# A cyclic order for five engines, rebuilt: attention pairs, routing steps and both remainder copies in an attention + mixture-of-experts kernel

## The chip, the cores and the metric

The kernel runs on one core of a Trainium2 chip. The metric is the device time of one execution, in microseconds (us). Names of engines: PE is TensorE (matrix products and transposes), DVE is VectorE, ACT is ScalarE, POOL is GpSimd, SP is SyncE, which here issues nearly all transfers.

## The reference

Attention with rotary positions over 8 batches, 8 heads, 576 tokens and 64 dimensions a head, then a layer in which each of the 4608 tokens goes through one of 8 experts.

```python
q_rot, k_rot = rotate(q), rotate(k)
scores = q_rot @ k_rot.T / sqrt(64)
scores = scores - scores.max(-1)
attn = exp(scores) / (sum(exp(scores)) + 1e-9)
x = (attn @ v) laid out as 4608 tokens x 512
logits = x @ w_gate                       # 8 experts
e = argmax(logits); g = softmax(logits)[e]
out = g * (relu(x @ w1[e]) @ w2[e])       # everything in float32
```

## The kernel before

Two heads make a **pair**; there are 32 pairs (`npair`), four to a batch. The attention part runs as a software pipeline. `PLAN` (line 26) is a list of steps `(token, offset)`; `window(w)` (line 769) walks it once and performs every token for pair `w - offset`. So one window holds one pair's worth of work, taken from up to seven neighbouring pairs. The last letter of a token is its engine (p PE, v DVE, a ACT, g POOL, d a transfer issued by SP). `chained_emit` (line 727) ties the instructions of each engine together in the order of the list, so that `PLAN`, read engine by engine, is the order in which each engine works. Every engine and SP's queue work strictly in order.

The tokens, in the order in which one pair goes through them:
- `FQd`, `FKd` fetch the pair's q and k (`fetch`, line 376). `paced` (line 368) makes such a load wait for the ACT instruction that stood last in the order.
- `RQg`, `RKg` rotate q and k on POOL (line 395, then the sum on line 396).
- `HQa`, `HKa` round q and k on ACT, `LQg`, `LKg` form the rests on POOL; `DHd`, `DLd` copy the halves of q across partitions.
- `cR` copies the last 64 columns of the rotated q into `zq` (line 409 is the helper's line of every copy), `DRd` swaps them across partitions.
- `S0p` to `S8p` are the nine score blocks on PE (six products each, line 459; S4, the remainder rows, line 454). They go into the PSUM tile `sp`, of which there are two.
- `M0v` to `M8v` on DVE copy a block out of PSUM, negated, and take its row maximum (line 471); `E0a` to `E8a` on ACT are the exponentials with their row sums (line 478).
- `TA0p`, `TA1p`, `TB0p`, `TB1p` transpose the exponentials on PE (line 496), `TRp` those of the remainder (lines 503, 507). Each fills one PSUM tile `tp`; there are two of these, handed out in turn to TR, the four T, the output block O and the products V.
- `cA0a` to `cB1a` copy the four T blocks to `PT` on ACT. TR is copied in two parts: `c1v` on DVE takes its first 256 columns to `PT`, `c2` the other 256 to `PR` (512 elements a partition each). `c3v` copies two small blocks out of O. c1 and c2, with c3, are the remainder copies.
- `V0p` to `V8p` multiply by v (lines 540, 542), `Uv` copies the result, `Op` (line 568) brings it to token rows and multiplies by the gate's weights, `X0v`, `X1v` (line 592) scale it into the batch's tile `xt`.
- `ZDd` moves a pair's remainder row sums across partitions (line 485); `RZv` on DVE sums and inverts the row sums (lines 145, 554) and so waits for `ZDd`.

Once a batch has its four pairs, **gating** (`gate`, line 620) routes its tokens: `gL` logits, `gM` maximum, `gD` difference (POOL, line 651), `gE` exponential (ACT, line 654), `gG`, `gW` weight, `gQ`, `gB`, `gO` one-hot, `gP` counts on PE inside O, `gR` ranks, `gU` (POOL, line 701), `gY` list positions. Then come five stores of the batch's rows (`gS0d` to `gS4d`, SP, line 671) and five scatters of the token lists (`gI0g` to `gI4g`, POOL, line 709). `GATE`, `STORES` and `LISTS` say after which token of which later window each of these goes.

From pair 28 on, `route_first` spreads the first steps of the expert schedule over the windows, `first_slots` loads three index lists through SP, the first expert's weights are loaded (lines 892, 894) and the first tokens gathered (line 322). As the pairs run out, the expert part begins: slots of 256 tokens with one expert each, PE at work all the time (lines 959 and 991). It takes the second half of the time.

Of the kernel before, what the change touches and what calls it, by code (L numbers as in the profile page):

```python
# [35 lines left out]
]  # L36
GATE = [
    ("gLv", 2, "G1"), ("gMv", 2, "G1"), ("gDg", 2, "RQg"), ("gEa", 2, "E6a"), ("gGv", 2, "G2"), ("gWv", 2, "G2"),
    ("gQv", 2, "G3"), ("gBv", 2, "G3"), ("gOv", 3, "G1"), ("gUg", 4, "RQg"), ("gYv", 4, "G2"),
]  # L40
STORES = (
    [
        ("gS0d", 3, "GS"), ("gS1d", 4, "GS"), ("gS2d", 5, "GS"), ("gS4d", 5, "ZDd"), ("gS3d", 6, "GS"),
    ],
    [
        ("gS0d", 3, "FQd"), ("gS1d", 3, "ZDd"), ("gS2d", 3, "FKd"), ("gS3d", 3, "DHd"), ("gS4d", 3, "DLd"),
    ],
)
LISTS = (
    [  # L50
        ("gI0g", 5, "GI"), ("gI1g", 6, "GI"), ("gI2g", 7, "GI"), ("gI3g", 8, "GI"), ("gI4g", 8, "LKg"),
    ],
    [
        ("gI0g", 4, "RKg"), ("gI1g", 5, "LQg"), ("gI2g", 5, "GI"), ("gI3g", 5, "RQg"), ("gI4g", 5, "LKg"),
    ],
)
W0 = -4
WARM = 80
RSTEP = ("M8v", "X0v", "M5v", "M1v", "Uv", "M6v", "M0v")
WSPLIT = (("TB0p", "cA1a"), ("HQa", "HKa"))  # L60
CHUNK = (0, 1, 3, 4, 2)
NR = 2
# [19 lines left out]
def kernel(  # L82
# [11 lines left out]
    B, H, S, D = v.shape  # L94
# [741 lines left out]
    WT = npair + max(off for tok, off in PLAN if tok[0] == "T")  # L836
# [94 lines left out]
    def keep(f, *a):  # L931
        chained_emit(lambda: f(*a), True)
# [103 lines left out]
    def early(i):  # L1036
        return {k: (lambda g=g: split1(g)) for g, k in enumerate(WSPLIT[i], 2 * i)}
# [168 lines left out]
```

## Time and profile before

| | |
|---|---|
| Median of 3 runs | 975.3 us (975.07 to 978.81) |
| The profiled execution | 973.34 us |
| Its span, first to last instruction | 971.2 us |
| PE, weight loads, DVE, ACT, POOL busy | 923.0, 778.2, 666.7, 665.9, 480.0 us |
| Mean granted TensorE clock | 0.971 of full speed |

The profile's summary adds up busy time over the whole span. The questions here are about one pair of some 13 us, so the views to read are those of a stretch: the table of waits, the table of windows, and the order of time on one engine. A row in order of time gives the start, the length, the engine, the line, the result and the operands with their shapes, how many instructions are merged, and in brackets how long the engine was idle before it and what released it. PE's instructions overlap, so the distance from one start to the next, not the length, is what a group costs PE.

### The profile page before, as it was taken

The page shows a single profiled execution, that of the slowest core. Times are in us where ns is not written, and L with a number is a line of the kernel's source. Part 1 is how long each engine was busy: PE and PEld are TensorE (multiplying, and loading weights), DVE is VectorE, ACT ScalarE, POOL GpSimd, SP SyncE. Part 2 cuts the span into 40 slices and gives each one's busy share as a digit, 9 for nine tenths or more (in the row PEclk, how much of TensorE's full clock was granted, in tenths as well). Part 3 has the DMA queues.
Part 4 walks back from the last instruction along what each step waited for, and adds up shares of the span by engine and source line. Part 5 has one row for each costly group of instructions (what it writes and reads, how often), then busy time and mean ns, then how long its engine had stood idle before and what let it go on. Part 6 is the DMA issues. An engine that isn't in the chain of part 4 may idle for free. (4 is left out here: it accounts for less than half of the span.)

```text
span 971.2 us, 25315 instructions
## 1 busy us (share of the span) xinstructions
PE 923.0 (95%) x9656; PEld 778.2 (80%) x9656; DVE 666.7 (69%) x1382; ACT 665.9 (69%) x1185; POOL 480.0 (49%) x335
## 2 busy tenths in 40 slices
PE   5799999999999999998999999999999999999997
PEld 4577777777777777765688999999999999997886
DVE  6557777777777777785478565666666666667987
ACT  2689999899998999887444445455445555456875
POOL 5977879998989889870224122222222111110111
PEclk7679999999999999999799999999999999999999
DMA  6656666676666766655312377414425311155991
GB/s 231 169 152 191 182 189 184 158 198 176 174 178 164 189 175 184 167 132 186 121 24 81 94 238 232 150 62 146 144 68 173 117 48 47 43 184 182 371 336 58
DMA packets 99827, 152.95 MB, mean 157 GB/s; under 512 B 28791, under 2 KB 62263, under 8 KB 99696
## 3 DMA queue, kind: packets, MB, share of 16 engines
q1 hardware_dynamic: 91408, 128.86, 45.6%
q0 software_dynamic: 8000, 21.20, 6.6%
q8 instruction: 79, 1.29, 0.6%
q10 hardware_dynamic: 288, 1.18, 0.3%
q14 instruction: 52, 0.43, 0.2%
HBM read 162.49 MB, written 23.80 MB: 192 GB/s over the span
## 5 line engine op out<-in xcount | busy, mean ns | idle before, releaser
L471 DVE TENSOR_SCALAR_CACHE_REDUCE pn<-sp 128x576 f32<-128x576 f32 x256 | 186.4, 746 | 34.5 <-PE sp L459 29.8
L478 ACT ACTIVATE pn<-pn,negm 128x576 f32<-128x576 f32 x256 | 195.1, 768 | 2.2 <-DVE pn L471 2.2
L459 PE MATMUL sp<-k,q 64*128 64x288 f32 x1536 | 168.0, 331 | 11.0 <-DMA q<-q 8.9
L959 PE MATMUL hp<-xh,w1h 128*128 128x256 f32 x544 | 154.4, 284 | 0.7 <-issue 0.4
L959 PE MATMUL hp<-xl,w1h 128*128 128x256 f32 x544 | 154.2, 283 | 0.0
L959 PE MATMUL hp<-xh,w1l 128*128 128x256 f32 x544 | 153.9, 283 | 0.0
L459 PEld LDWEIGHTS sp<-k,q 64*128 64x128 f32 x1536 | 118.5, 198 | 26.3 <-issue 17.5
L898 DVE TENSOR_TENSOR w2l<-r,w2h 128x1024 fp32r<-128x1024 f32 x92 | 111.7, 1231 | 36.3 <-ACT w2h L897 31.1
L1001 POOL DMA_INDIRECT out_dram<-y,gi x34 | 34.4, 1011 | 204.0 <-DVE y L152 181.2
L542 PE MATMUL tp<-PT,vn 128*64 128x320 f32 (+1 forms) x1024 | 134.5, 414 | 0.0
L409 ACT COPY PT<-tp 128x1024 f32<-128x1024 f32 x128 | 125.0, 1013 | 13.5 <-PE tp L496 12.3
L991 PE MATMUL yp<-w2h,hh 128*128 128x512 f32 x320 | 126.5, 395 | 0.0
L991 PE MATMUL yp<-w2h,hl 128*128 128x512 f32 x320 | 124.9, 390 | 0.0
L991 PE MATMUL yp<-w2l,hh 128*128 128x512 f32 x320 | 124.8, 390 | 0.0
L898 DVE TENSOR_TENSOR w1l<-r,w1h 128x1024 fp32r<-128x1024 f32 x96 | 113.0, 1217 | 4.3 <-ACT w1h L897 3.6
L542 PEld LDWEIGHTS tp<-PT,vn 128*64 128x64 f32 x1024 | 71.8, 139 | 48.8 <-issue 6.8
L959 PEld LDWEIGHTS hp<-xh,w1h 128*128 128x128 f32 x544 | 104.3, 192 | 2.4 <-DVE lpi L145 0.6
L959 PEld LDWEIGHTS hp<-xh,w1l 128*128 128x128 f32 x544 | 104.3, 192 | 0.6
L959 PEld LDWEIGHTS hp<-xl,w1h 128*128 128x128 f32 x544 | 104.3, 192 | 0.6 <-issue 0.5
L395 POOL TENSOR_TENSOR qk<-qk,rotq 128x1152 f32<-128x1152 f32 x31 | 82.1, 2648 | 45.4 <-DMA qk<-in_qk_dram 42.2
L496 PE MATMUL tp<-cst,pn 64*128 64x64 f32 x2048 | 91.2, 231 | 13.7 <-ACT pn L478 8.5
L927 ACT ACTIVATE hh<-hp 128x512 fp32r<-128x512 f32 x68 | 40.6, 598 | 90.0 <-PE hp L959 86.2
(192 smaller groups left out, 1775.6 us busy)
## 6 DMA issues: line engine op xcount, KB each, us to landing
r<-in_moe_w_dram SPq DMA_DIRECT2D x192, 512.0 KB
qk<-in_qk_dram SPq DMA_DIRECT2D x64, 576.0 KB
q<-q SPq DMA_DIRECT2D x128, 128.0 KB
x_dram<-xt SPq DMA_DIRECT2D x32, 288.0 KB
vn<-in_v_dram SPq DMA_DIRECT2D x32, 256.0 KB
xlist<-mark SPq DMA_DIRECT2D x8, 289.0 KB
x_dram<-xt SPq DMA_DIRECT2D x8, 144.0 KB
zq<-zq SPq DMA_DIRECT2D x64, 16.0 KB
```

What stands on the lines that cost most here:

```text
L395: e.tensor_tensor(out=x, in0=x, in1=rot, op=ALU.mult)
L409: (nc.scalar.copy if eng == "a" else nc.vector.tensor_copy)(out=o, in_=i)
L459: nc.tensor.matmul(sp[:, u, 0:HS], lhsT=st["q"][r, int(h != u), qp, i * P:(i + 1) * P], rhs=st["k"][r, kp, h], start=(i_ == 0), stop=(i_ = ...
L471: nc.vector.tensor_scalar(out=scores(st, n, j), in0=st.pop(("S", j))[:, :, 0:HS], scalar1=-1.0, scalar2=None, op0=ALU.mult, op1=ALU.min, a ...
L478: nc.scalar.activation(out=t, in_=t, func=AF.Exp, bias=st["negm"][:, j:j + 1], scale=-1.0, accum_out=zs[n % 4][:, CHUNK[i], h, 0:1])
L496: nc.tensor.transpose(tp[:, b, c:c + 64], pns[n % 2][r, i, k:k + P], ident[r, r])
L542: nc.tensor.matmul(o, lhsT=st["vn"][:, h, s % 4, :], rhs=st["PT"][:, h, s % 4, x:x + w], start=(s % 4 == 0), stop=False)
L898: nc.vector.tensor_tensor(out=lo, in0=src, in1=hi.bitcast(F32), op=ALU.subtract)
L927: nc.scalar.activation(out=hh, in_=hp, func=AF.Relu)
L959: m = nc.tensor.matmul(hp[:, fi], lhsT=w[:, dc, fs], rhs=x[:, dc], start=(i == 0), stop=(i == len(prods) - 1))
L991: m = nc.tensor.matmul(yp[t], lhsT=h[:, fi, ts_], rhs=w[:, fi], start=(g == 0 and fi == 0 and i == 0), stop=(g == FQ - 1 and fi == 1 and i ...
L1001: sc = nc.gpsimd.indirect_dma_start(out=out, out_offset=bass.IndirectOffsetOnAxis(ap=si[:, t:t + 1], axis=0), in_=y, in_offset=None, bound ...
```

## The change

All of it is in the tables of the order, but for two lines near the end of the kernel.
- `PLAN` is a new order. c2 is now `c2v`, so that DVE does both copies out of TR, and `cR` is now `cRa`, on ACT. Offsets that differ: `RQg` and `RKg` -3 instead of -4, `LKg` -2 instead of -3, `ZDd` 0 instead of 1, and E2, E3 and E8 traded between -1 and -2.
- The five places in `PLAN` that were kept only for gating (`G1`, `G2`, `G3`, `GI`) are gone; gating's steps hang on other tokens, and batch 6, the last but one, has places of its own (`GATE[1]`). `gU` and `gY` moved into `LISTS`, whose second set now begins at batch 4 instead of 5.
- `RSTEP`, the tokens after which `route_first` advances, is new.
- The gather of the second expert slot's tokens is issued one window later, and the last batch's gating, which follows the pipeline, takes `GATE[0]`'s order.

```diff
 PLAN = [
+    ("FQd", -4), ("RQg", -3), ("cA0a", 0), ("cB1a", 0), ("TRp", 0), ("HQa", -3), ("LKg", -2), ("S3p", -2), ("c2v", 0),
+    ("DHd", -3), ("M3v", -2), ("VPd", -2), ("c1v", 0), ("Op", 2), ("X0v", 2), ("S8p", -2), ("E2a", -1), ("E5a", -1),
+    ("S0p", -2), ("cRa", -3), ("X1v", 2), ("FKd", -4), ("V0p", 1), ("V1p", 1), ("V2p", 1), ("V3p", 1), ("E6a", -1),
+    ("RKg", -3), ("c3v", 2), ("M8v", -2), ("LQg", -3), ("E3a", -2), ("V4p", 1), ("V5p", 1), ("V6p", 1), ("V7p", 1),
+    ("E7a", -1), ("DLd", -3), ("RZv", 1), ("HKa", -3), ("S4p", -2), ("V8p", 1), ("M0v", -2), ("GS", 0), ("M4v", -2),
+    ("S2p", -2), ("TB0p", -1), ("Uv", 1), ("S7p", -2), ("ZDd", 0), ("E0a", -1), ("E1a", -1), ("E8a", -2), ("M2v", -2),
+    ("TA1p", -1), ("M7v", -2), ("S1p", -2), ("M1v", -2), ("E4a", -1), ("DRd", -3), ("cB0a", -1), ("TA0p", -1),
+    ("cA1a", -1), ("S6p", -2), ("TB1p", -1), ("S5p", -2), ("M6v", -2), ("M5v", -2),
 ]
-    ("gLv", 2, "G1"), ("gMv", 2, "G1"), ("gDg", 2, "RQg"), ("gEa", 2, "E6a"), ("gGv", 2, "G2"), ("gWv", 2, "G2"),
-    ("gQv", 2, "G3"), ("gBv", 2, "G3"), ("gOv", 3, "G1"), ("gUg", 4, "RQg"), ("gYv", 4, "G2"),
+        ("gLv", 2, "E3a"), ("gMv", 2, "HKa"), ("gDg", 3, "V3p"), ("gQv", 3, "RKg"), ("gBv", 3, "M8v"), ("gOv", 3, "E3a"),
+        ("gEa", 3, "M4v"), ("gGv", 3, "TA0p"), ("gWv", 4, "VPd"),
...
+        ("gUg", 5, "E3a"), ("gYv", 5, "M0v"), ("gI0g", 6, "M0v"), ("gI1g", 6, "M0v"), ("gI2g", 7, "FQd"),
+        ("gI3g", 9, "M1v"), ("gI4g", 9, "M1v"),
...
-                for name, off_, at in GATE + STORES[b == B - 2] + LISTS[b >= B - 3]:
+                for name, off_, at in GATE[b == B - 2] + STORES[b == B - 2] + LISTS[b >= B - 4]:
...
-    gather(1, 2)
...
         window(w, early(1) if w == WT else {}, lambda tok, n: n < npair - 1 or tok[:-1] not in LATE)
+        if w == WT:
+            gather(1, 2)
```

How the instructions stand on three engines, before and now. First ACT, from the copies of one pair's transposes (`PT<-tp`) through the exponentials (`pn`, `pr`) to gating's exponential (`gate_ex`); `q` and `k` are the rounded halves. Before:

```order
L409 COPY PT<-tp 128x2x2x4x64 x3
L409 COPY PR<-tp 128x2x4x64
L409 CAST q_5847<-yq 128x512
L409 COPY PT<-tp 128x2x2x4x64
L478 ACTIVATE pr_129,z_119<-pr_129,negm 128x576
L478 ACTIVATE pn_146,z_122<-pn_146,negm 128x576 x2
L478 ACTIVATE pn_145,z_119<-pn_145,negm 128x576 x4
L409 CAST k_5942<-yk 128x576
L478 ACTIVATE pn_145,z_119<-pn_145,negm 128x576
L654 ACTIVATE gate_ex<-dl 128x5x8
```

Now:

```order
L416 COPY PT<-tp 128x2x2x4x64 x4
L416 CAST q_5061<-yq 128x512
L485 ACTIVATE pn_146,z_122<-pn_146,negm 128x576 x2
L416 COPY zq_126<-yq 128x64
L485 ACTIVATE pn_146,z_122<-pn_146,negm 128x576
L485 ACTIVATE pn_145,z_113<-pn_145,negm 128x576
L485 ACTIVATE pn_146,z_122<-pn_146,negm 128x576
L416 CAST k_5150<-yk 128x576
L661 ACTIVATE gate_ex<-dl 128x5x8
```

The four copies out of PSUM stand together, `PR<-tp` (c2) has left ACT, `zq<-yq` (cR) has come to it.

Then DVE, from the last score blocks of a window (`pn,negm<-sp`) over the copies out of TR (`PT<-tp`, `PR<-tp 128x2x4x64`) and the two X (`xt<-tp,rz`) to RZ (`rz<-z`), in a window with gating steps. Before:

```order
L471 TENSOR_SCALAR pn_145,negm<-sp 128x576 x4
L409 COPY PT<-tp 128x2x4x64
L471 TENSOR_SCALAR pn_146,negm<-sp 128x576 x2
L592 TENSOR_TENSOR xt_81<-tp,rz 128x5x72 x2
L409 COPY zq_125<-yq 128x64
L471 TENSOR_SCALAR pn_146,negm<-sp 128x576
L640 TENSOR_REDUCE L<-xt_81 128x40
L645 TENSOR_REDUCE mx<-L 128x5
L145 TENSOR_REDUCE rz<-z_113 128x10
```

Now:

```order
L478 TENSOR_SCALAR pn_146,negm<-sp 128x576 x5
L416 COPY PR<-tp 128x2x4x64
L478 TENSOR_SCALAR pn_145,negm<-sp 128x576
L416 COPY PT<-tp 128x2x4x64
L599 TENSOR_TENSOR xt_80<-tp,rz 128x5x72 x2
L684 SCALAR_TENSOR_TENSOR gate_eq<-dl,cst 128x5x8
L416 COPY PR<-tp 64x64 x2
L478 TENSOR_SCALAR pn_145,negm<-sp 128x576
L688 TENSOR_REDUCE bs<-gate_eq 128x5
L155 TENSOR_TENSOR oh<-gate_eq,bs 128x40
L152 TENSOR_REDUCE rz<-z_116 128x10
```

c2 comes first, one score block stands between it and c1, and cR is gone.

Last, SP's queue where the pairs end: the first expert's weights (`r_0` to `r_3`), v of the last pair (`vn`, `vr`), a store of rows (`x_dram<-xt`) and the row sums that pair 29 waits for (`z_116`). Before:

```order
L892 DMA r_0_7876<-in_moe_w_dram 128x4x256
L892 ISA
L892 DMA r_1_7879<-in_moe_w_dram 128x4x256
L385 DMA vn<-in_v_dram 128x2x256
L387 DMA vr_136<-in_v_dram 64x64 x2
L892 ISA
L892 DMA r_2_7882<-in_moe_w_dram 128x4x256
L892 ISA
L892 DMA r_3_8193<-in_moe_w_dram 128x4x256
L671 DMA x_dram<-xt_80 64x1x1152
L485 DMA z_116<-z_116 64x1
```

Now:

```order
L310 DMA gi_84<-xlist 128x2x1
L678 DMA x_dram<-xt_81 64x576
L492 DMA z_116<-z_116 64x1
L305 TENSOR_LOAD sched
L305 ISA x2
L899 ISA
L899 DMA r_0_8166<-in_moe_w_dram 128x4x256
L899 ISA
L899 DMA r_1_8169<-in_moe_w_dram 128x4x256
```

The row sums of pair 29 stood behind four weight loads and now stand ahead of all of them, right after the index loads.

## Rows read from the trace of the kernel before

**Rows 1.** Waits, 97.92 to 423.96 us: engine, tile, line, releaser; total, times, longest.

```profile
POOL qk L395 <- DMA qk<-in_qk_dram: 26.3, 17, 3.4
...
ACT PR L409 <- DVE PT L409: 22.7, 24, 1.6
...
PE tp L568 <- ACT PR L409: 7.6, 22, 1.0
...
POOL q L417 <- ACT q L409: 5.7, 8, 0.7
...
PE tp L496 <- ACT pn L478: 5.0, 6, 1.3
ACT gate_ex L654 <- POOL dl L651: 4.4, 5, 1.3
```

**Rows 2.** Windows: length, busy PE, PEld, DVE, ACT, POOL; clock, DMA share, GB/s.

```profile
97.92:423.96 326.04, 312.26 (x4861) 242.49 (x4861) 241.98 (x711) 294.87 (x607) 284.75 (x181) 1.00 0.66 178
...
452.46:467.84 15.38, 11.24 (x144) 8.37 (x145) 3.29 (x9) 9.74 (x20) 0.73 (x1) 0.80 0.92 319
467.84:478.75 10.91, 10.91 (x82) 7.09 (x83) 2.74 (x10) 3.79 (x4) 2.30 (x3) 0.65 0.40 104
```

**Rows 3.** Order of time on PE, one pair without gating, from O to O.

```profile
260.12 0.65 PE L459 MATMUL sp<-k,q 64*128 64x288 f32 x6
260.66 1.34 PE L568 MATMUL tp<-iw,uT 64*128 64x72 f32 x20
...
261.86 1.04 PE L459 MATMUL sp<-k,q 64*128 64x288 f32 x12
262.83 4.10 PE L542 MATMUL tp<-PT,vn 128*64 128x256 f32 x32
...
270.96 0.65 PE L459 MATMUL sp<-k,q 64*128 64x288 f32 x6
271.45 0.41 PE L503 MATMUL tp<-cst,pr 64*128 64x64 f32 x8
...
271.91 0.65 PE L459 MATMUL sp<-k,q 64*128 64x288 f32 x6
...
272.86 0.65 PE L459 MATMUL sp<-k,q 64*128 64x288 f32 x6
273.69 1.34 PE L568 MATMUL tp<-iw,uT 64*128 64x72 f32 x20 [0.18 <-ACT PR L409]
```

**Rows 4.** Order of time on DVE, the end of the same pair.

```profile
271.65 0.76 DVE L471 TENSOR_SCALAR_CACHE_REDUCE pn<-sp 128x576 f32<-128x576 f32 x1 [0.18 <-PE sp L459]
...
272.34 0.69 DVE L409 COPY PT<-tp 128x512 f32<-128x512 f32 x1
```

**Rows 5.** Order of time on ACT, the end of the same pair.

```profile
269.34 2.87 ACT L409 COPY PT<-tp 128x1024 f32<-128x1024 f32 x3
273.06 0.59 ACT L409 COPY PR<-tp 128x512 f32<-128x512 f32 x1 [0.84 <-DVE PT L409]
273.54 0.62 ACT L409 CAST q<-yq 128x512 fp32r<-128x512 f32 x1
```

**Rows 6.** Order of time, a pair with gating's exponential, ACT and PE.

```profile
174.21 0.24 ACT L654 ACTIVATE gate_ex<-dl 128x40 f32<-128x40 f32 x1 [1.26 <-POOL dl L651]
...
175.26 0.71 PE L496 MATMUL tp<-cst,pn 64*128 64x64 f32 x16 [1.34 <-ACT pn L478]
```

**Rows 7.** Order of time where the pairs end: SP, DVE, PE.

```profile
453.64 0.64 SPq L485 DMA_DIRECT2D z<-z  x1
...
461.25 0.17 DVE L145 TENSOR_REDUCE rz<-z 128x10 f32<-128x20 f32 x1 [6.27 <-DMA z<-z]
...
462.13 1.97 PE L496 MATMUL tp<-cst,pn 64*128 64x64 f32 x32 [3.55 <-DVE PR L409]
...
470.66 6.43 PE L542 MATMUL tp<-PT,vn 128*64 128x256 f32 x32
```

**Rows 8.** Windows, four microseconds of the same place.

```profile
458.00:462.00 4.00, 0.58 (x10) 0.13 (x5) 0.69 (x4) 0.62 (x2) 0.00 (x0) 0.97 1.01 370
```

More of the change, by code (lines that the diff above doesn't have):

```diff
@@ L26 @@
 PLAN = [
[9 rows of a table removed]
-]
-GATE = [
-    ("gLv", 2, "G1"), ("gMv", 2, "G1"), ("gDg", 2, "RQg"), ("gEa", 2, "E6a"), ("gGv", 2, "G2"), ("gWv", 2, "G2"),
-    ("gQv", 2, "G3"), ("gBv", 2, "G3"), ("gOv", 3, "G1"), ("gUg", 4, "RQg"), ("gYv", 4, "G2"),
-]
+    ("FQd", -4), ("RQg", -3), ("cA0a", 0), ("cB1a", 0), ("TRp", 0), ("HQa", -3), ("LKg", -2), ("S3p", -2), ("c2v", 0),
[7 rows of a table added]
+]
+GATE = (
+    [
+        ("gLv", 2, "E3a"), ("gMv", 2, "HKa"), ("gDg", 3, "V3p"), ("gQv", 3, "RKg"), ("gBv", 3, "M8v"), ("gOv", 3, "E3a"),
+        ("gEa", 3, "M4v"), ("gGv", 3, "TA0p"), ("gWv", 4, "VPd"),
+    ],
+    [
+        ("gLv", 2, "c3v"), ("gMv", 2, "M8v"), ("gDg", 3, "RQg"), ("gEa", 3, "HQa"), ("gQv", 3, "c2v"), ("gBv", 3, "M3v"),
+        ("gOv", 3, "c1v"), ("gGv", 3, "X0v"), ("gWv", 3, "X1v"),
+    ],
+)
 STORES = (
     [
-        ("gS0d", 3, "GS"), ("gS1d", 4, "GS"), ("gS2d", 5, "GS"), ("gS4d", 5, "ZDd"), ("gS3d", 6, "GS"),
+        ("gS0d", 4, "M0v"), ("gS1d", 4, "M4v"), ("gS2d", 5, "TB1p"), ("gS3d", 6, "M4v"), ("gS4d", 6, "M4v"),
     ],
     [
-        ("gS0d", 3, "FQd"), ("gS1d", 3, "ZDd"), ("gS2d", 3, "FKd"), ("gS3d", 3, "DHd"), ("gS4d", 3, "DLd"),
+        ("gS0d", 3, "FKd"), ("gS1d", 3, "DLd"), ("gS2d", 3, "ZDd"), ("gS3d", 3, "DRd"), ("gS4d", 4, "FQd"),
     ],
@@ L50 @@
     [
-        ("gI0g", 5, "GI"), ("gI1g", 6, "GI"), ("gI2g", 7, "GI"), ("gI3g", 8, "GI"), ("gI4g", 8, "LKg"),
-    ],
-    [
-        ("gI0g", 4, "RKg"), ("gI1g", 5, "LQg"), ("gI2g", 5, "GI"), ("gI3g", 5, "RQg"), ("gI4g", 5, "LKg"),
+        ("gUg", 5, "E3a"), ("gYv", 5, "M0v"), ("gI0g", 6, "M0v"), ("gI1g", 6, "M0v"), ("gI2g", 7, "FQd"),
+        ("gI3g", 9, "M1v"), ("gI4g", 9, "M1v"),
+    ],
+    [
+        ("gUg", 4, "RKg"), ("gYv", 4, "RZv"), ("gI0g", 5, "RQg"), ("gI1g", 5, "LKg"), ("gI2g", 5, "RKg"),
+        ("gI3g", 5, "LQg"), ("gI4g", 6, "RQg"),
     ],
@@ L58 @@
 WARM = 80
-RSTEP = ("M8v", "X0v", "M5v", "M1v", "Uv", "M6v", "M0v")
+RSTEP = ("M3v", "X0v", "c3v", "M0v", "Uv", "M7v", "M6v")
 WSPLIT = (("TB0p", "cA1a"), ("HQa", "HKa"))
@@ L1085 @@
     last = gate(B - 1, False)
-    for name, *_ in GATE + STORES[0] + LISTS[0]:
+    for name, *_ in GATE[0] + STORES[0] + LISTS[0]:
         last[name[:-1]](name[-1])
```

9 rows, old and new, of the table PLAN are left out of this document.

## The prediction, made before the changed kernel ran

> **What bounds the kernel now.** I read the table of windows first. From 97.92 to 423.96 us, 24 pairs, PE is busy 312.26 of 326.04 us, ACT 294.87, POOL 284.75, DVE 241.98 [rows 2]: PE comes first, and only its 13.8 us of idle time, with what each stop costs around it, can be won there. The expert part is PE without a gap and is not touched; whatever the change is worth must come from the pairs and from the place where they end.
>
> The table of waits says what PE waits for. O waits for ACT's copy c2: 22 times, 7.6 us. A T waits for an exponential: 6 times, 5.0 us [rows 1]. Behind the first is a second wait: ACT's c2 waits for DVE's c1, 24 times, 22.7 us [rows 1]. Both copies read the same tile TR. Behind the waits of T stands gating: ACT's `gate_ex` waits for POOL's `gD`, 4.4 us in 5 batches [rows 1].
>
> The order of time of a pair without gating shows the first. DVE's c1 runs from 272.34 to 273.03 [rows 4]; c2 starts at 273.06 after 0.84 us idle and ends at 273.65 [rows 5]; O starts at 273.69 [rows 3]. The last score block started at 272.86, so O came 0.83 us behind it; a pair earlier, with c2 in time, it came 0.54 us behind (260.12 to 260.66) [rows 3]. **One pair thus loses 0.29 us of its 13.03**, although only 0.18 is recorded as idle.
>
> A pair with gating: ACT stops 1.26 us at `gate_ex`, the exponential behind it is late, and T on PE stops 1.34 us [rows 6].
>
> Where the pairs end: the row sums of pair 29 are issued at 453.64 [rows 7], behind the first expert's weight loads in SP's order, the transfers run at 370 GB/s [rows 8], and RZ waits for them until 461.25, 6.27 us, with everything behind it on DVE. PE stops 3.55 us until 462.13 [rows 7]. The granted clock, 0.97 while PE stands nearly idle [rows 8], is 0.80 and 0.65 in the two windows that hold the stop and what follows [rows 2]; that is the lower of the two levels, 1.2 instead of 2.4 GHz, for part of each. A pair's V takes 6.43 us there [rows 7] against 4.10 [rows 3].
>
> **The change part by part.**
>
> *c2 to DVE.* ACT loses c2 (0.48 us from its start to the next, 273.06 to 273.54) and the wait of 0.84 before it [rows 5]. O now needs only the T blocks' copies on ACT. PE, DVE and ACT must be followed to see what is late next. In the new order PE does, from the last score block S5: S5 0.49 (270.96 to 271.45), TR 0.46, S3 0.54, O 1.20, S8 and S0 0.97, then V [rows 3]: V starts 3.66 us after S5. V takes over TR's PSUM tile and so waits for c2 and c1. DVE meanwhile: M5 starts 0.69 after S5 and takes 0.69 to the next start (271.65 to 272.34) [rows 4]; c2 0.69 as c1, which has the same 512 elements out of the same tile, or at most the 0.76 of a score block's row, which I take; M3 0.69; c1 0.69. That ends at 3.52. V is not delayed, by 0.14 us. ACT does its four T copies in one run, each behind one PE block; PE spends 0.95 us on a score block and a group of transposes (0.49 + 0.46) [rows 3], ACT 0.96 on a copy (2.87 for three) [rows 5], so the two keep step and O meets no late copy. The gain lies between 0 (a T copy is late instead) and 0.29 a pair: the recorded 7.6 us, and 0.11 more in each of 22 stops, 2.4, together 10.0. I take **9.0 us**, near the upper end, since the walk above finds each producer ready. The two pairs ahead of 97.92 add **0.5**.
>
> *cR to ACT.* DVE gets rid of a small copy, ACT gains one of 64 columns. Its price lies between `gate_ex`'s 0.24 us for 40 columns [rows 6] and the rounding of q with 512 columns, 0.62 [rows 5]; I take 0.26, near the smaller. ACT falls by 0.48 and the 0.84 wait and rises by 0.26, so it keeps about a microsecond a pair to spare: cost nothing. If that cover went, the price would be 0.26 a pair.
>
> *Gating.* `gD` now has its input a window ahead, and `gE` stands half a window behind it; `gQ`, `gB` and `gO` follow in the stretch in which DVE has idle time, `gG` and `gW` one step at a time. So ACT does not stop at `gate_ex`, and the six waits of T, 5.0 us, should go; the ends are 0 and 5.0, and as the counts on PE stay and `gW` now stands between M3 and c1, whose slack is 0.14, I take **4.0**. The list scatters come in twos behind `LQ`; POOL waits for the fetch there today (26.3 us in 17 stops [rows 1]), and that idle time hides them. Stores and fetches on SP keep their number; the fetch of q stands first in the window and its rotation one window later, which is more lead than now.
>
> *The end of the pairs.* The row sums of pair 29 stand ahead of the weight loads in SP's queue, and their token one window earlier. RZ then finds them in time. The ends are 0 (another late transfer) and 3.55 of idle PE with 2.33 of V at the lower clock (6.43 − 4.10), 5.9. I take **4.5**: the stop goes, the clock is kept for part of what follows. The second slot's gather, a window later, is hidden behind the first slot's products; the new order of the last batch's gating is hidden behind PE in the expert part; the route steps on DVE in the windows ahead of the end stay as many. If their cover went, each would cost what it takes on DVE, under a microsecond or two in all.
>
> Over the 24 pairs the granted clock was 1.00 [rows 2] in spite of the 28 stops of PE [rows 1], so I count on it where PE only makes short stops. By the Trainium skill (TensorE: Matmul & The Clock Gate, "A second HAM failure mode: psum-queue depth-cycling") short idle gaps between groups of matmuls, as PSUM tiles cycle, can bring the clock down again and again; by that rule the end would bring 3.55 only, and the sum would be 17.0.
>
> The sum: 9.0 + 0.5 + 4.0 + 4.5 = 18.0. The profiled execution took 973.34 us; less 18.0 is 955.3. The median shown, 975.3, lies 2.0 above that execution, so I forecast **957 us** for a median.
>
> **The rivals.**
>
> *POOL becomes the bound* (or one of the other halves fails). POOL's 284.75 us of work, with the 26.3 it waits for fetches and the 5.7 for ACT's q [rows 1, 2], make 316.8 us over the 24 pairs. If these waits stay and now decide, the stretch wins 9.3 instead of 13.0; with nothing won at the end the time is 975.3 − 9.8, about 965. For it: POOL is the nearest engine to full once PE's waits are gone. Against: POOL's product is needed nearly a window later than it is ready.
>
> *The wait moves to V.* If c2 on DVE takes longer than c1, or M5 comes later, V waits for c1. The slack is 0.14 us; 0.43 more eats the whole 0.29 a pair, and 0.75 a pair would eat all 18 us over 32 pairs. Between those the time is within 5 us of 975, say 973. Against: c2 has the size and the source of c1.
>
> *POOL waits longer, and the kernel is slower.* The place is the fetch of q ahead of `RQ`. `LK` now stands behind the next pair's `RQ` and ahead of S3 of the same window, so that a late fetch reaches PE through LK. POOL has 41.3 us beside its work in 24 pairs, 1.72 a pair; today's fetch waits take 1.1 of that, the longest was 3.4 [rows 1]. Above 1.72 a pair the stretch gets longer than now. At 2.5 it would take 284.75 + 60 = 344.8, 18.7 more; with the 4.5 at the end won, 975.3 + 14, about 989. Against it: the fetch has more lead, and the paced load waits for an ACT step that comes no later.
>
> *The clock falls at the end all the same.* Where the score blocks run out, PE waits between every T and the next for a copy of 0.96 us [rows 5]; if that is enough to lower the clock, the end brings the stop's 3.55 [rows 7] instead of 4.5, and the time is 958.
>
> **How the numbers follow.** Half a per cent, 4.9 us, is about what a measurement of this kernel can tell from no change. Forecast 0.50 and its cousin with the clock 0.10; POOL or one half failing, 965, 0.22; the wait moves to V, 973, 0.11; slower, 989, 0.07. The upper ends of all terms (10.0 + 0.6 + 5.0 + 5.9 = 21.5) give 953.8; starts and the expert part may shift by some microseconds too, so the range begins at 949. It ends at 969, beyond the 965 case. Faster by over 0.5% (below 970.4): 0.82; within: 0.11; slower: 0.07.
>
> **What would show it.** Right: the distance from O to O in a pair without gating near 12.74 us (13.03 − 0.29), no line in the table of waits in which O waits for `PR`, none in which `gate_ex` waits for `dl`, RZ's wait for `z` gone, V of the last pairs nearer 4.1 us. Wrong: V (line 549 of the new kernel) waits for DVE's `PT` copy; the first S of a window waits for POOL's `k`; POOL's waits for `qk` above 1.7 us a pair; or PE's idle time as large as now.

## The result, and the profile after

| | before | after |
|---|---|---|
| Median of the runs on one chip | 975.54 us (975.07 to 978.81) | 948.84 us (947.84 to 948.96) |
| Ratio | | 0.9717, interval 0.9695 to 0.9739 |
| Profiled execution, its span | 973.34, 971.2 us | 948.83, 946.8 us |
| Mean granted clock | 0.971 | 0.978 |

The kernel became 2.8% faster. The forecast was 957.0, the range 949 to 969: the sign was right, and the time lies 0.16 us below the range. To see where the time went, I cut both spans at the starts of the output blocks O on PE and set each stage beside the forecast. O(0) is the first O, O(31) the last.

| stage | before | after | difference | forecast |
|---|---|---|---|---|
| start to O(0) | 71.85 | 66.17 | -5.68 | 0 |
| O(0) to O(2) | 26.07 | 25.09 | -0.98 | -0.5 |
| O(2) to O(26), 24 pairs | 326.04 | 315.30 | -10.74 | -13.0 |
| O(26) to O(31), the end of the pairs | 66.74 | 58.05 | -8.69 | -4.5 |
| O(31) to the end, experts | 480.50 | 482.19 | +1.69 | 0 |
| sum | 971.2 | 946.8 | -24.4 | -18.0 |

Two stages gave more than forecast, one less, one lost a little. The 24 pairs hide two errors that partly cancel. A pair without gating (a clean pair) went from 13.04 to 12.54 us, 0.49 to 0.50 instead of 0.29, which is 24 x 0.49 = 11.8 where 9.0 was forecast; but what gating's windows take above that clean period was to fall by 4.0 and rose, from 13.2 us to 14.2 (13.2 in a second profile of the same kernel). That the sum, 10.74, lies near the forecast of 13.0 is luck.

The windows of after, with the columns of [rows 2]: the 24 pairs, then the four stretches from O to O behind them.

```profile
91.26:406.56 315.30, 309.52 (x4864) 244.85 (x4860) 263.09 (x711) 288.10 (x607) 285.73 (x183) 0.99 0.66 184
406.56:422.80 16.24, 14.70 (x201) 11.61 (x202) 14.59 (x42) 12.26 (x26) 8.44 (x7) 0.89 0.32 73
422.80:435.39 12.59, 12.32 (x199) 9.57 (x195) 11.48 (x40) 10.63 (x24) 0.26 (x1) 1.00 0.29 64
435.39:446.70 11.31, 9.68 (x144) 7.12 (x144) 4.63 (x17) 9.29 (x20) 2.06 (x2) 1.00 1.01 327
446.70:454.12 7.42, 7.42 (x82) 4.96 (x82) 5.33 (x14) 1.84 (x2) 3.03 (x3) 1.00 0.84 277
```

In the 24 pairs PE's idle time fell from 13.8 us to 5.8. The last two rows answer to the last two of [rows 2]: 15.38 became 11.31 and 10.91 became 7.42, and the clock that was 0.80 and 0.65 is 1.00.

The table of waits of after over the 24 pairs (in us: total, times, longest):

```profile
ACT PT L416 <- PE tp L503: 23.3, 29, 1.3
POOL qk L402 <- DMA qk<-in_qk_dram: 11.5, 8, 2.1
...
POOL gate_rk L708 <- DVE gate_rk L155: 5.1, 2, 2.6
...
PE sp L466 <- DVE pn L478: 2.6, 5, 0.7
...
PE tp L503 <- DVE uT L416: 2.2, 4, 1.7
...
PE tp L575 <- ACT PT L416: 0.3, 1, 0.3
```

Against [rows 1], all three waits that the prediction named are gone: no O waits for `PR`, no T for an exponential, and `gate_ex` no longer waits for `dl`. New is that score blocks (line 466) wait for DVE, and T for DVE's copy `uT`. POOL's wait for the fetch of q fell from 26.3 us to 11.5, while its work stayed the same (285.73).

### The profile page after: what moved, and what is told of

It is laid out like the page before. It is cut to its first block, busy times and chain, and to the rows that moved or that the text cites. A ratio compares the mean times of both kernels' runs of the same rounds, so it can differ in the third digit from the quotient of the medians.

```text
span 946.8 us, 25292 instructions
## 1 busy us (share of the span) xinstructions
PE 910.2 (96%) x9656; PEld 775.8 (82%) x9656; DVE 689.5 (73%) x1383; ACT 655.9 (69%) x1184; POOL 481.0 (51%) x335
## 4 chain that ended last, share of the span: by engine, by line
PE 73%; issue 10%; DVE 7%; DMA 5%; ACT 3%; POOL 1%; SPq 1%; another core or an unknown queue 1%; POOLq 0%; DVEq 0%
PE hp L966 18%; PE yp L998 17%; PE sp L466 11%; PE tp L549 11%; PE tp L503 7%; DMA out_dram<-y,gi 3%; PE tp L575 3%; DVE pn L478 2%; PE sp L461 2%; PE xps L921 1%; PE tp L547 1%; ACT pn L485 1%; DVE oh L155 1%; POOL out_dram L1008 1%; DMA q<-q 1%
## 5 line engine op out<-in xcount | busy, mean ns | idle before, releaser
L478 DVE TENSOR_SCALAR_CACHE_REDUCE pn<-sp 128x576 f32<-128x576 f32 x256 | 190.2, 752 | 31.5 <-PE sp L466 27.3
L549 PE MATMUL tp<-PT,vn 128*64 128x320 f32 (+1 forms) x1024 | 131.4, 409 | 0.5 <-DVE oh L155 0.4
L904 ACT CAST w2h<-r 128x1024 fp32r<-128x1024 f32 x92 | 94.8, 1043 | 5.5 <-PE tp L575 2.5
L904 ACT CAST w1h<-r 128x1024 fp32r<-128x1024 f32 x96 | 95.6, 1051 | 0.0
```

The lines of the kernel that those rows point to most:

```text
L478: nc.vector.tensor_scalar(out=scores(st, n, j), in0=st.pop(("S", j))[:, :, 0:HS], scalar1=-1.0, scalar2=None, op0=ALU.mult, op1=ALU.min, a ...
L549: nc.tensor.matmul(o, lhsT=st["vn"][:, h, s % 4, :], rhs=st["PT"][:, h, s % 4, x:x + w], start=(s % 4 == 0), stop=False)
L904: nc.scalar.copy(out=hi, in_=src)
```

## The experiments

### Does the engine of c2 matter, or its place in the order?

*Theory:* O waited for a c2 that came late on ACT; on DVE it comes in time. *Rival:* what frees O is where TR stands. PSUM tiles are handed out in turn to two: in the old order a T block stands between TR and O, so O takes over the tile that c1 and c2 must empty; in the new one TR is the last, and V takes that tile, an output block and score blocks later. Two more offsets differ and bear on this: TB1 went from 0 to -1, ahead of TR, and cA0 from -1 to 0. (Of the exponentials only E2 and E3 traded offsets; E8 stayed at -2. The stores have new places as well.)

**The kernel before with c2 on DVE.**

```diff
-("TB1p", 0), ("FQd", -4), ("c2a", 0), ("S2p", -2), ("ZDd", 1)
+("TB1p", 0), ("FQd", -4), ("c2v", 0), ("S2p", -2), ("ZDd", 1)
```

> The kernel before with one word changed: c2 on VectorE, in its old place behind c1; order, gating and end as before. Theory (the order frees O, not the engine): VectorE does c2 right behind c1, so it ends where ACT's ended, within 0.1 us, and O still waits for it: O to O stays near 13.0 us in a pair without gating; ACT, rid of c2 and of its wait, lets the six T waits on exponentials shrink, so the 24 pairs win 0 to 5 us and the time is 970 to 975. If the 5.7 us that the changed kernel wins before its first O also come from ACT no longer waiting for c1, they show here too, and the time is near 967. Rival (it is the engine that counts): O to O falls to about 12.6 and the time to about 958.

Ratio to before 1.0003 (0.9978 to 1.0028); clean pairs of 13.06 us. Its table of waits has the same wait of O under another name:

```profile
PE tp L568 <- DVE PR L409: 8.4, 24, 0.6
PE tp L496 <- ACT pn L478: 3.2, 6, 0.8
```

Its 24 pairs took 323.08 us, 3.0 less than before's, in the gating windows, where T's waits fell from 5.0 to 3.2; the times don't show it.

**The kernel after with c2 back on ACT.** In the first form batch 6's `gQ`, which hung on the token `c2v`, was left out, so of it only the pairs are used; the second has `gQ` on `c2a`.

```diff
-("S3p", -2), ("c2v", 0),
+("S3p", -2), ("c2a", 0),
...
-("gQv", 3, "c2v")
+("gQv", 3, "c2a")
```

> The changed kernel with c2 back on ACT, in its new place; cR stays on ACT. Theory (the place of TR behind the last T block frees O, not the engine of c2): O does not wait for c2; ACT goes from 12.0 us of work a pair to about 12.5 of 12.54, so O to O is 12.54 to 12.7 us and the time lies 0 to 6 us above the changed kernel's, 949 to 955. Rival (it is the engine): c2 waits for c1 again, the casts and exponentials behind it on ACT are late, O to O is 12.83 or more, 956 or slower.

> The changed kernel with c2 back on ACT and everything else in place, gating of batch 6 too (in the run before that one step of batch 6, gQ, hung on the name of c2 and was left out, so that its expert part was not the same). Theory: which engine does c2 is worth nothing; O to O in a pair without gating is 12.5 us as in that run, and the ratio to the kernel before lies within 0.004 of the changed kernel's own (0.972 and 0.977 in its two comparisons). Rival: it is the engine after all, and the ratio is 0.982 or more.

The first form took 945.8 us, with 12.52 from O to O. The second took 945.75, ratio 0.9776 (0.9752 to 0.9800) beside a before of 968.55, with 12.52 again. So the clean pair is 13.04 (ACT) and 13.06 (DVE) in the old order, 12.52 (ACT) and 12.54 (DVE) in the new: the order is worth 0.5 us a clean pair, the engine nothing. In the gating windows the engine may count: the 24 pairs took 310.95 and 312.43 us with c2 on ACT in the new order, 315.30 and 314.35 with it on DVE; but the ratio, 0.9776, lies at one of after's two (0.9717 and 0.9773) and above the other, so that no gain of it shows in the time. That it is the PSUM tile through which the order acts fits the wait that changes only its name in the first run; it wasn't tried by itself.

### The end of the pairs: one token?

**The kernel before with the row sums' transfer one window earlier.**

```diff
-("c2a", 0), ("S2p", -2), ("ZDd", 1), ("HQa", -3),
+("c2a", 0), ("S2p", -2), ("ZDd", 0), ("HQa", -3),
```

> The kernel before with the transfer of the remainder row sums one window earlier (offset 0 for 1), nothing else. Theory: the stop of 3.55 us and the V at the lower clock (2.33 us) both come from RZ's wait behind the weight loads; the time falls by 5.9 us to about 969.5, and from the last O of batch 6 on the windows look like those of the changed kernel. Rival 1: the whole 8.7 us that the changed kernel wins at the end come from this token: about 967. Rival 2: the transfer is late for another reason, or the end's gain comes from gating's new places: less than 2 us, above 973.

963.62 us beside 970.32, ratio 0.9925 (0.9903 to 0.9948). O(26) to O(31) fell from 66.74 to 59.30 us; the two windows with the stop, in the columns of [rows 2], became

```profile
452.17:463.26 11.09, 9.61 (x144) 6.69 (x144) 3.19 (x9) 9.75 (x20) 0.85 (x1) 1.00 0.97 318
463.26:470.68 7.42, 7.42 (x82) 4.96 (x82) 2.73 (x10) 3.70 (x4) 2.29 (x3) 1.00 0.91 306
```

This one token carries 7.4 of the 8.7 us that the end won, and it would have been had without the rest.

### Where gating's gain went

In the profile of after the one-hot of gating, eight small DVE operations, takes ten times as long as before (the median). The rows of its tile give minimum, median and maximum in ns. The kernel before:

```profile
L148 DVE TENSOR_TENSOR oh<-gate_eq,bs x8: 191/194/196, 128.5 to 505.7; 128x40 bf16<-128x40 f32 x8
```

The kernel after:

```profile
L155 DVE TENSOR_TENSOR oh<-gate_eq,bs x8: 192/2060/2534, 120.6 to 478.5; 128x40 bf16<-128x40 f32 x8
```

One of them in order of time in after: DVE, POOL and PE.

```profile
171.69 2.53 DVE L155 TENSOR_TENSOR oh<-gate_eq,bs 128x40 bf16<-128x40 f32 x1
174.14 0.16 DVE L152 TENSOR_REDUCE rz<-z 128x10 f32<-128x20 f32 x1
...
171.51 2.65 POOL L402 TENSOR_TENSOR qk<-qk,rotq 128x1152 f32<-128x1152 f32 x1
...
175.26 0.66 PE L466 MATMUL sp<-k,q 64*128 64x288 f32 x6 [0.60 <-DVE pn L478]
```

It begins just after POOL's product and ends with it (174.22 and 174.16); the next score row comes late, and PE stops. The profile shows this as busy DVE time and not as a wait, so no table of waits has it. Before, the same instruction stood in the gap in which POOL waited for the fetch of q:

```profile
128.49 0.19 DVE L148 TENSOR_TENSOR oh<-gate_eq,bs 128x40 bf16<-128x40 f32 x1
...
129.36 2.64 POOL L395 TENSOR_TENSOR qk<-qk,rotq 128x1152 f32<-128x1152 f32 x1 [2.14 <-DMA qk<-in_qk_dram]
```

By the Trainium skill (SBUF — State Buffer, "Who interferes with whom") a DVE instruction with both inputs in SBUF contends with a GpSimd instruction that reads SBUF, and the loser is blocked for the whole of it. These rows agree. *Theory A:* this lock costs the gating windows their gain. *Theory B:* POOL's list scatters fill it up, and its k comes late to the first score block.

**The kernel after with the one-hot half a window later.**

```diff
-("gBv", 3, "M8v"), ("gOv", 3, "E3a"),
+("gBv", 3, "M8v"), ("gOv", 3, "M0v"),
```

> The changed kernel with one token moved: gating's one-hot (gO) stands behind M0 instead of behind E3's place, in front of the score block M4, for which VectorE waits some 2 us anyway. Theory: the one-hot took 1.3 to 2.5 us in batches 0 to 5 because VectorE's two-input instruction waited for GpSimd's running rotation, and so held M0 and M4 back by 0.7 to 0.9 us in each of five windows. Behind M0 this wait is hidden: the five windows fall from 13.3 to 13.5 us to about 12.55, and the time by 3.5 to 4.5 us to about 944.7. Rival: those windows are long because of gating's other steps (exponential, sums): no change, 948 to 949.

948.71 us, ratio 0.9770 (0.9746 to 0.9794): not to be told from after's, and not the 944.7 of the theory. One of the gating windows fell from 13.38 to 12.54, three others stayed at 13.13 to 13.18, since the one-hot there is still 1.66 us long, and in one window S3 waited 4.00 us for POOL's `k`. The 24 pairs won 2.6 us, the start, where this edit touches nothing, took 2.8 more. A is half right, and B is there as well.

**The kernel after with the scatters spread.**

```diff
-("gI0g", 6, "M0v"), ("gI1g", 6, "M0v"), ("gI2g", 7, "FQd"), ("gI3g", 9, "M1v"), ("gI4g", 9, "M1v"),
+("gI0g", 6, "M0v"), ("gI1g", 7, "M0v"), ("gI2g", 8, "M0v"), ("gI3g", 9, "RQg"), ("gI4g", 9, "M0v"),
...
-("gI0g", 5, "RQg"), ("gI1g", 5, "LKg"), ("gI2g", 5, "RKg"), ("gI3g", 5, "LQg"), ("gI4g", 6, "RQg"),
+("gI0g", 5, "RQg"), ("gI1g", 5, "RKg"), ("gI2g", 5, "LQg"), ("gI3g", 6, "RQg"), ("gI4g", 6, "LQg"),
...
-LISTS[b >= B - 4]
+LISTS[b >= B - 3]
```

> The changed kernel with the five list scatters of a batch spread over windows, one or at most two at a place and a POOL step between any two, and the second set of places again from batch 5 on, as in the kernel before. Theory: where three or four scatters stand back to back, PE's results reach VectorE and ACT 0.3 to 1.9 us late (S4 to M4 1.17 to 1.83 us there, 0.88 elsewhere), which costs 0.3, 1.0, 0.7 and 0.9 us in four windows and 3.6 in the one of 16.13 us. Spread, S4 to M4 is 0.88 everywhere, and the time falls by 4 to 7 us, to 942 to 945. Rival: the lateness has to do with the stores or the fetch in the same windows, not with the scatters: no change, 948 to 949, and the 16.13 us window stays.

945.19 us, ratio 0.9739 (0.9712 to 0.9765) beside the same before as the last kernel; the 24 pairs 310.04. The worst window fell from 16.13 to 12.55 us. The windows of the one-hot stayed at 12.85 to 13.92.

**The kernel after once more**, nothing edited, to see what is chance of one execution.

> The changed kernel once more, nothing edited, for a second profile beside the other runs. In its first profile M4 came 1.2 to 1.8 us after S4 in one window of each of batches 0 to 3 (0.88 elsewhere), which cost 0.3 to 1.0 us a window, and in the window of 16.13 us PE's results reached VectorE and ACT 1.7 us late. If that belongs to the program, the same windows show it again; if it is chance of an execution, they do not, and the window of 16.13 us stays long all the same, now with S3 waiting for GpSimd's k, since GpSimd has four scatters, two rotations and k to do in it. Time within 1 us of 948.8 on the same chip, a little off on another.

950.26 us, ratio 0.9773 (0.9717 to 0.9830) beside a before of 971.86; span 949.3, 24 pairs 314.35. What lies above the clean period is now 13.2 us, and its parts are plain: gating's counts inside O, 6 x 0.475 = 2.9; the three windows with a long one-hot, 4.3; one window in which POOL is full and the next, 5.8; 0.2 elsewhere. In the first profile score rows also came up to 0.9 us late in the windows with three scatters; the second has none of that, and what it was stays open. The full window, POOL and PE, then it and the next in the table of windows:

```profile
355.71 0.99 POOL L716 DMA_INDIRECT xlist<-tid,lpi  x1 [0.17 <-issue]
357.00 0.97 POOL L716 DMA_INDIRECT xlist<-tid,lpi  x1 [0.30 <-issue]
...
364.59 1.41 POOL L433 TENSOR_TENSOR k<-yk,k 128x576 fp32r<-128x576 f32 x1
...
366.05 0.40 PE L466 MATMUL sp<-k,q 64*128 64x288 f32 x2 [3.70 <-POOL k L433]
```
```profile
349.48:366.29 16.81, 13.02 (x205) 10.01 (x202) 10.60 (x30) 14.61 (x32) 15.49 (x12) 1.00 0.65 180
366.29:380.40 14.11, 14.11 (x202) 10.95 (x202) 10.14 (x29) 9.54 (x20) 13.88 (x9) 0.88 0.54 133
```

Five scatters (not four, as I had expected) of 1.0 us and their gaps in one window give POOL more than a clean period has. S3 waits 3.70 us for `k`, and in the window behind the stop PE is busy throughout and yet takes 1.57 us more, at a granted clock of 0.88 (the lower level, 1.2 GHz, for part of it).

**The kernel after with all five scatters in one window for batches 0 to 3.**

```diff
-("gI0g", 6, "M0v"), ("gI1g", 6, "M0v"), ("gI2g", 7, "FQd"), ("gI3g", 9, "M1v"), ("gI4g", 9, "M1v"),
+("gI0g", 6, "M0v"), ("gI1g", 6, "M0v"), ("gI2g", 6, "M0v"), ("gI3g", 6, "M0v"), ("gI4g", 6, "M0v"),
```

> The changed kernel with all five list scatters of batches 0 to 3 in one place, behind M0, instead of two, one and two in three windows. Theory (GpSimd is the bound where scatters pile up): five scatters are 6.5 us between the rest of q and the next rotation in a window in which GpSimd's other work is some 11.1 of 12.54 us, so k's rest is late and S3 waits for GpSimd's k, 3 to 5 us in each of four windows, as in the window of 16.13 us; the windows that held the other scatters lose what they paid. In sum 8 to 15 us slower, 957 to 964. Rival (the scatters delay PE's results in proportion to their number): M4 comes 2 us or more after S4 there, each window pays 1 to 2 us, S3 never waits for k, and the time is 950 to 953.

```profile
PE sp L466 <- POOL k L433: 7.0, 5, 1.7
```

The wait is the one that B expected, once a batch, but with 1.4 us instead of three to five. The time, 950.81 us (ratio 0.9769, 0.9709 to 0.9828), misses the expected 957 to 964 and lies in the rival's range, though S3 does wait for `k`, which the rival excluded; the kernel after itself took 950.26 on the same chip. Four windows grew to 13.94 to 14.48 us, 1.4 to 1.9 above the clean pair. The one-hot behind them was short (0.20 us in batches 1 to 5), presumably because POOL was elsewhere in its order by then. Two of its windows became clean (12.54), the other two took 14.14 and 14.12 with PE busy throughout, behind the stop and at the lower clock for part of it; one of them, in the columns of [rows 2]:

```profile
221.05:235.19 14.14, 14.14 (x202) 10.85 (x202) 10.01 (x31) 10.80 (x24) 13.90 (x8) 0.88 0.48 119
```

**Both repaired.** The scatters spread as above, the one-hot behind `RK`, POOL's last work for a while, and the route steps at places where POOL was idle or at the scatters.

```diff
-("gBv", 3, "M8v"), ("gOv", 3, "E3a"),
+("gBv", 3, "RKg"), ("gOv", 3, "RKg"),
...
-RSTEP = ("M3v", "X0v", "c3v", "M0v", "Uv", "M7v", "M6v")
+RSTEP = ("M0v", "M2v", "M7v", "M1v", "M6v", "M5v")
```

> The changed kernel with three edits: scatters spread as in the run that spread them; gating's gB and gO right behind gQ, where GpSimd's rest of q has just ended and a scatter stands next; the schedule's steps behind M0 and in the second half of the window, where GpSimd is idle or scattering. Theory (two-input instructions of VectorE wait for a running GpSimd tensor instruction): the one-hot takes 0.2 us instead of 1.3 to 2.5, the windows with it fall to 12.6, the window of the schedule's steps from 16.2 to about 13, and the time to 936 to 940. Rival: the schedule comes later by half a window, so the first expert's indices and gather are late and the expert part gives back what the pairs win: 943 to 946.

940.85 us, ratio 0.9685 (0.9629 to 0.9742), beside 950.26 for the kernel after on the same chip; the 24 pairs 305.87, the one-hot's median 0.20 us. Three windows were left: 13.42, where batch 0's one-hot still takes 2.60 us, 14.04, where S3 waits 0.73 for `k`, and 16.04, where a route step `f1t` takes 2.19 us, until POOL's k is done. The last kernel moves the last batches' scatters behind `LQ` and `LK`:

```diff
-("gI0g", 5, "RQg"), ("gI1g", 5, "RKg"), ("gI2g", 5, "LQg"), ("gI3g", 6, "RQg"), ("gI4g", 6, "LQg"),
+("gI0g", 5, "LQg"), ("gI1g", 6, "LKg"), ("gI2g", 6, "LKg"), ("gI3g", 6, "LKg"), ("gI4g", 6, "LKg"),
```

> The combined kernel with the five scatters of batch 5 behind the last k of GpSimd instead of in front of it (one behind the rest of q, four behind k). Theory: in the combined kernel S3 still waited 0.7 us for k in the window of 14.04 us, and a step of the schedule stood 2.2 us on VectorE until that k was done (window of 16.04 us). Behind k the scatters delay nothing: these two windows fall to about 13.0 and 13.5 us, the 24 pairs to about 305 us, the time by 2 to 4 us to 937 to 939 on the chip of that run, and with a ratio to the kernel before of 0.963 to 0.967. Rival: the schedule ends later because its scatters do, the first weights' indices come late and the end loses it again: ratio 0.968 as the combined kernel.

937.99 us (936.46 to 939.29), ratio 0.9682 (0.9658 to 0.9705) beside a before of 968.55. The ratio is the rival's 0.968, not the expected 0.963 to 0.967, and doesn't tell this kernel from the last one (0.9685). The trace does: the two windows fell to 13.04 and 12.73 as expected, the 24 pairs to 304.65. What the experts took was 484.25 us instead of 482.78, but it varies by as much in the kernel after (482.19 and 484.26), so that the rival's loss at the end is neither shown nor excluded. No chip ran this kernel and the kernel after; the latter with c2 on ACT took 945.75 beside the same before. PE's only recorded wait from 91 to 420 us, in the window of batch 0's one-hot (2.31 us), is

```profile
PE sp L461 <- DVE pn L478: 0.5, 1, 0.5
```

### The start

The start was costed at nothing and gave 5.7 us. The two windows of it that differ, before (S4 to S4 on PE):

```profile
32.65:46.52 13.87, 11.68 (x138) 9.14 (x139) 8.11 (x21) 11.67 (x24) 12.52 (x8) 0.67 0.40 101
46.52:65.07 18.55, 15.86 (x171) 11.99 (x171) 9.11 (x28) 16.18 (x36) 14.07 (x8) 0.72 0.65 182
```

and after:

```profile
33.85:45.09 11.24, 9.53 (x140) 8.11 (x138) 8.41 (x23) 11.24 (x24) 11.08 (x8) 0.77 0.57 155
45.09:59.72 14.63, 13.02 (x171) 9.93 (x171) 9.17 (x26) 14.63 (x33) 14.47 (x9) 0.88 0.69 191
```

ACT is busy without a gap in after; before it has gaps, and T waited for exponentials 3.5 us in all. *Theory:* the exponentials stand further ahead of the T that needs them. *Rival:* it is the copies, which stand in one run. Two more lie in the rows. The clock: for almost as many products (309 and 311) PE was busy 27.54 us before and 22.55 after, at 0.67 and 0.72 against 0.77 and 0.88, and ACT's copies before waited 0.3 and 0.7 us for PE's T blocks in each of the two windows; no run separates this from the order. And ACT's c2, which in the start before waits 3.5 us for c1; with c2 on DVE in the old order (the first run above) ACT has neither the copy nor the wait, and the first O stood at 71.43 all the same.

**The kernel after with one exponential, E5, moved from ACT's second to its last.**

```diff
-("E2a", -1), ("E5a", -1), ("S0p", -2)
+("E2a", -1), ("S0p", -2)
...
-("S2p", -2), ("TB0p", -1), ("Uv", 1), ("S7p", -2), ("ZDd", 0), ("E0a", -1), ("E1a", -1), ("E8a", -2)
+("S2p", -2), ("E0a", -1), ("E1a", -1), ("E8a", -2), ("E4a", -1), ("E5a", -1), ("TB0p", -1), ("Uv", 1)
...
-("M1v", -2), ("E4a", -1), ("DRd", -3)
+("M1v", -2), ("DRd", -3)
```

> The changed kernel with one exponential moved: E5, which the first T block of the next pair needs, is ACT's last exponential of a window instead of its second; nothing else moves on any engine. Theory on the start (before its first O the changed kernel wins 3 to 6 us because a T block never waits for an exponential that ACT has only just done, so that ACT, the fullest engine there, runs without a gap): with E5 last, T waits for it again in the start, and part of the gain is lost: first O 1.5 to 4 us later than 66.2 to 67.3 (the six profiles but one), while in the pairs behind O to O stays 12.54, since there E5 still ends half a microsecond ahead of T. Time 1 to 4 us above the changed kernel's, ratio to the kernel before 0.976 to 0.981. Rival: the start is won by the rotations' or copies' places: first O stays at 66 to 67.5 and the ratio at 0.972 to 0.977.

It took 956.9 us, ratio 0.9837 (0.9795 to 0.9879) beside 973.44, the first O at 73.28 instead of 66.17; the clean pair became 12.72 us, where I had expected 12.54. From 30 to 75 us its PE waited

```profile
PE tp L503 <- ACT pn L485: 7.3, 2, 3.8
```

**The kernel before with its exponentials in the other succession,** each token of the nine replaced in its place, and `gE` on the token that now stands where it was.

```diff
 the E tokens of PLAN, in order
-E4 E2 E8 E7 E0 E1 E3 E6 E5
+E2 E0 E1 E3 E8 E7 E6 E5 E4
```

> The kernel before with its nine exponentials in another order on ACT: E2, E0, E1, E3, which its first T block needs, first, then E8, E7, E6, E5, and E4, which no T block needs, last instead of first; gating's exponential stays where it was between them. The other side of the same question. Theory: T's waits on exponentials (3.5 us in the start, 5.0 in the 24 pairs) shrink by a half or more; the first O comes 1 to 3 us earlier than 71.4 to 72.2, the 24 pairs win 1 to 3 us, O to O without gating stays 13.04, since O still waits for c2; ratio 0.994 to 0.998. Rival: ACT's order within the nine changes nothing, since the copies behind them are late then: ratio 1.00.

It took 972.88 us, ratio 1.0000 (0.9973 to 1.0027), with the first O at 72.96. Over the pairs its T waits for copies instead:

```profile
PE tp L568 <- ACT PR L409: 6.6, 21, 0.6
PE tp L496 <- ACT PT L409: 5.0, 6, 1.9
```

In its start T still waits for exponentials, 4.8 us instead of 3.5, now above all ahead of the second T block of a pair (from 30 to 73 us):

```profile
PE tp L496 <- ACT pn L478: 4.8, 3, 2.6
```

So the lead of the exponentials is needed: one that is late costs the whole gain of the start, and more than I had expected. In the pairs of the old order another succession is worth nothing, since the copies behind the exponentials are late then. For the start the last run decides nothing, because it moved T's wait there and didn't remove it. Whether the lead alone makes the gain, or the run of copies or the clock with it, is not shown. All kernels with the old order have their first O at 71.4 to 73.0, those with the new at 66.0 to 68.9 but for the one with E5 last.

## Why the prediction was right and wrong

**c2, 9.0 and 0.5.** Right: O's wait is gone, and V took no new one, so that "the wait moves to V" did not come true. Wrong in size, 11.8 and 1.0. The step that failed is "a pair earlier, with c2 in time, it came 0.54 us behind". That O was held as well; the yardstick was not a free one. Its c2 on ACT shows it:

```profile
260.02 0.59 ACT L409 COPY PR<-tp 128x512 f32<-128x512 f32 x1 [0.47 <-DVE PT L409]
```

It ended at 260.61, 0.05 us ahead of the O at 260.66; in the late pair c2 ended at 273.65, 0.04 ahead of the O at 273.69. (Nor do the upper ends agree: 0.29 a pair is 7.0 in 24 pairs, and the 10.0 came from recorded waits that average 0.35.) The weight loads say the same: before, the pair I took as in time, and the late one,

```profile
260.66 1.19 PEld L568 LDWEIGHTS tp<-iw,uT 64*128 64x128 f32 x20
...
273.69 1.19 PEld L568 LDWEIGHTS tp<-iw,uT 64*128 64x128 f32 x20 [0.42 <-ACT PR L409]
```

after, a clean pair, weight loads and products:

```profile
193.59 1.20 PEld L575 LDWEIGHTS tp<-iw,uT 64*128 64x128 f32 x20
```
```profile
193.23 0.64 PE L466 MATMUL sp<-k,q 64*128 64x288 f32 x6
193.70 1.23 PE L575 MATMUL tp<-iw,uT 64*128 64x72 f32 x20
...
194.80 1.03 PE L466 MATMUL sp<-k,q 64*128 64x288 f32 x12
195.76 4.10 PE L549 MATMUL tp<-PT,vn 128*64 128x256 f32 x32
```

Before, O's first weights were loaded only as O began (260.66 in both rows); now they are in 0.11 us ahead. O follows the score block by 0.47 us instead of 0.83, and the next score block follows O by 1.10 instead of 1.20 [rows 3]: 0.46 of the 0.50. The credit was misplaced too: the prediction gave it to "c2 to DVE", and the four kernels above give it to the order.

**Gating, 4.0.** The waits it named, 5.0 of T behind 4.4 of `gate_ex`, are gone, and gave nothing net. Two steps failed. "Follow in the stretch in which DVE has idle time" looked only at DVE; the one-hot was blocked by POOL there, 4.3 us in three windows of the second profile. "That idle time hides them", of the scatters, does not hold for the window with five, 5.8 us with the clock; for two or three in a window it holds in the second profile, and the first is open. This is the rival "POOL becomes the bound", in one window instead of on average: POOL's busy time over the stretch did not rise, so the mean could not show it.

**The end, 4.5.** Right in mechanism, measured 8.7, above its upper end of 5.9. SP now issues the row sums ahead of the weights, and RZ doesn't wait; SP, DVE, PE in order of time, after:

```profile
432.63 0.59 SPq L492 DMA_DIRECT2D z<-z  x1
434.22 4.88 SPq L899 DMA_DIRECT2D r<-in_moe_w_dram  x4
```
```profile
440.14 0.17 DVE L152 TENSOR_REDUCE rz<-z 128x10 f32<-128x20 f32 x1
```
```profile
443.06 1.48 PE L503 MATMUL tp<-cst,pn 64*128 64x64 f32 x32 [0.39 <-DVE uT L416]
...
448.37 4.10 PE L549 MATMUL tp<-PT,vn 128*64 128x256 f32 x32
```

The step that was mis-sized is the clock: the upper end counted it for V only, 2.33 us, but it had slowed the other products of the two windows too. They became 15.38 + 10.91 - 11.31 - 7.42 = 7.56 us shorter. For the same 226 products PE was busy 17.10 us instead of 22.15, 5.05 less; its idle time fell by the other 2.51, less than the stop's 3.55, since after has short stops of its own. The rival "the clock falls at the end all the same" did not come: PE stops for 0.2 to 0.4 us, the clock is 1.00, V takes 4.10. The rule of the Trainium skill weighed in the prediction (TensorE: Matmul & The Clock Gate, on psum-queue depth-cycling) thus did not show here.

**Costed at nothing.** The start gave 5.7 (5.3 in the second profile): the failed step is that the sum put the start at nothing and the working never opened a view of it, though the range allowed it "some microseconds"; ACT runs without a gap there now, and one exponential out of place cost the whole gain. The route steps on DVE, at nothing or "under a microsecond or two", cost more than before: two of them meet POOL in the window 406.56 to 422.80, which is 16.24 us long against 15.14 before (17.22 in the second profile), 3.7 above the clean pair against 2.1. DVE and POOL in it:

```profile
410.65 1.24 DVE L155 TENSOR_TENSOR f1p<-f1c,f 1x8 f32<-1x8 f32 x1
...
413.79 1.98 DVE L159 TENSOR_SCALAR d<-d 1x8 f32<-1x8 f32 x1
```
```profile
410.58 1.29 POOL L424 TENSOR_TENSOR q<-yq,q 128x512 fp32r<-128x512 f32 x1
...
414.31 1.42 POOL L433 TENSOR_TENSOR k<-yk,k 128x576 fp32r<-128x576 f32 x1
```

Eight numbers take 1.98 us and end with POOL's k (415.77 and 415.73). PE then stops 1.37 us, and the clock is at the lower level from 418 to 421. cR on ACT cost 0.23 us, as estimated (0.26).

**The experts, 0.** They take 1.1 to 3.8 us longer in every kernel with the new tables, and 0.1 to 0.3 in those with the old. About 396 us behind the last O, where the small slots begin, PE stops 1.10 us before, released by ACT's sequencer, and 3.07 after, released by weights that ACT rounds. Why is open.

**The time.** The errors were -5.7 (start), -4.2 (end), -0.5, +2.3 (pairs), +1.7: -6.4 in the span. The 2.0 that I added for a median above the profiled execution was not needed either, since after's median is its profile's time.

## What to carry to other kernels

Before an engine move is credited with the end of a wait, ask which buffer is handed over there and to whom: here the order did it, and the move nothing. A wait that is to be removed may be cover for something else; look at what runs beside each small two-input DVE operation on GpSimd, and put it behind GpSimd's last long one. A small transfer that many wait for belongs ahead of the big loads in its queue, and the fill and the drain of a pipeline want a view of their own, because the steady pair doesn't show them.

## What the runs showed of the hardware

A DVE operation on 128x40 or even 1x8 numbers took 1.2 to 2.6 us instead of 0.15 to 0.2 when it met a GpSimd product, and ended with it within 0.1 us; the profile counts it as DVE busy. An operation without two inputs was hit as well (`d<-d`, a tensor by a number, 1.98); it began during a scatter and ended with the product behind it. A GpSimd scatter of 128 rows keeps POOL 1.0 us, with 0.15 to 0.30 between two.
